# A gated linear attention with an MLP on one core: phase kept as wrapped 16-bit turns, gate preparation in two stages, and a list-scheduled order on all engines but Pool

## Chip, cores and metric

One core of one Trainium2 chip. The metric is the device time of one execution in microseconds (us). The engines are called PE (matrix multiply), DVE (VectorE), ACT (ScalarE), POOL (GpSimd) and SP (the queue that issues most loads). "Busy" and "idle" are read from a hardware profile of one execution.

## The reference, cut to what matters

```
B, H, S, D = 4, 8, 768, 48
mag   = sqrt(a_re^2 + a_im^2);  scale = min(mag, 0.999) / (mag + 1e-6)
a     = (a_re + i a_im) * scale                  # complex gate per position and channel
for t in range(S):
    State = a[t][:, None] * State + outer(k[t], v[t])    # complex 48x48 state per head
    y[t]  = q[t] @ real(State)
x   = y with heads side by side                   # (4, 768, 384)
out = x + relu(layernorm(x) * g_ln @ w_ch1) @ w_ch2      # 384 -> 1536 -> 384
```

The kernels do this in 24 chunks of 128 positions (6 per batch), three chunks to a "group", so eight groups. With the gate in polar form, the product of gates from one position to another is the exponential of a difference of cumulative log magnitudes `l` and a rotation by a difference of cumulative angles `th`. A group's gate preparation makes `e`, `en` (the exponentials of the cumulative logs and of their negatives), `sin` and `cos` of the cumulative angle, and the stacked operands `ks`, `qs` = k or q, times `en` or `e`, times `cos` or `sin`. Attention and the MLP then run on PE.

## The kernel before

The parts that the change touches:

```python
ctx.enter_context(tc.manual_schedule())     # each engine runs in the order of writing

def merge(*lists):                          # one step: attention of chunk n, a third of the
    ...                                     # preparation of the next group, a third of an MLP

# preparation of group g, all of it within the three steps before the group is used
L  = [le1, le2, le3]                        # ACT: w=ln(are), rinv=exp(-w); DVE: r=aim*rinv, r2=r*r
                                            # ACT: u=ln(1+r2); DVE: l=min(0.5u+w, cap)+eps
L += [lambda c=c: le4(c) for c in range(GC)]   # PE: lps=u_f^T l; ACT: e=exp(lps), en=exp(-lps)
L += [decay, tr1]                           # chunk totals; ACT: other table set, th=arctan(r)
L += [lambda c=c: tr2(c) for c in range(GC)]
L += [qk, tr3]                              # POOL: ke=k*en, qe=q*e; ACT: sin, cos
L += [lambda c=c: stack(c) for c in range(GC)]

def tr2(c):                                 # phase in turns, wrapped to [-0.5, 0.5]
    nc.tensor.matmul(ps, lhsT=u_th, rhs=th, start=True, stop=(car is None))
    if car is not None:
        nc.tensor.matmul(ps, lhsT=one_th, rhs=car, start=False, stop=True)
    nc.vector.tensor_scalar(out=n, in0=ps, scalar1=MAGIC, scalar2=MAGIC,
                            op0=ALU.add, op1=ALU.subtract)         # round to whole turns
    nc.vector.tensor_tensor(out=st["f"][:, c], in0=ps, in1=n, op=ALU.subtract)
    ... nc.gpsimd.tensor_tensor(out=nxt, in0=car, in1=th, op=ALU.add)   # running sum of angles
# tr3: af = f & 0x7FFF (DVE); sin = Sin(2 pi f), cos = Sin(pi/2 - 2 pi af) (ACT)

def transp(which):                          # "ks" and "qs"
    ... nc.vector.tensor_copy(out=t, in_=ps)
def mm1(jp):                                # first MLP layer, one double-bank PSUM tile
    ps = ph.tile([C, 2, 512], FP32, tag="h", name="hps")            # ph has one buffer
    ... six matmuls, then nc.scalar.activation(out=st["h"][:, ts(jp, 2)], in_=..., func=AF.Relu)
```

## Time and profile before

| before | |
|---|---|
| median of 4 runs | 347.40 us (345.75 to 348.66) |
| busy, of a span of 345.4 us | PE 215.6, DVE 206.4, ACT 167.9, POOL 93.6 us |
| first transposes of ks on PE | 30.4 us |
| time between the groups' sin activations, from 131 us on | 34 to 39 us |

The page of the kernel before: its span, the busy time of each engine, the busy tenths of PE, DVE and of PE's granted clock in 40 slices of the span, and the chain that ended last by engine.

```profile
span 345.4 us, 4940 instructions
PE 215.6 (62%) x1917; PEld 141.9 (41%) x1917; DVE 206.4 (60%) x424; ACT 167.9 (49%) x254; POOL 93.6 (27%) x115
PE   0041027644635754689568596789467949979884
DVE  1438066997896458837983568456955875743021
PEclk9999998855956788689868967688969989999999
PE 40%; DVE 29%; ACT 14%; SPq 6%; DMA 4%; POOL 3%; issue 2%; DVEq 0%
```

No engine is above two thirds. PE is hardly busy for the first six slices (52 us). Its granted clock is full there (9 in every slice) and at the end, and reduced in most slices between (down to 5). The chain that ended last goes from engine to engine; nothing is a bottleneck by its work. The list of waits says what the engines stood behind (engine and line, what it waited for: us in total, times, longest):

```profile
POOL v L104 <- PE tps L251: 49.6, 2, 26.4
PE lps L213 <- DVE l L206: 56.5, 8, 18.4
PE tp L315 <- DVE ks L291: 19.5, 8, 6.0
DVE w1b L153 <- DMA w1b<-in_moe_w_ch_dram: 8.5, 1, 8.5
```

PE waits for the beginning of the preparation (l) and again for its end (ks), once in each of the eight groups. DVE stood 8.5 us at the start behind a weight that no work of that moment needed. The costs of lines that the change touches, from the groups of instructions (busy us, mean ns of one | idle before, releaser):

```profile
L257 DVE TENSOR_TENSOR f<-tps,n 128x384 f16<-128x384 f32 x24 | 13.4, 558 | 0.8
L317 DVE COPY qsT<-tp 96x1024 bf16<-96x1024 bf16 x24 | 16.4, 684 | 15.0 <-PE tp L315 15.0
L204 DVE SCALAR_TENSOR_TENSOR l<-u,w 128x1152 f16<-128x1152 f16 x8 | 10.8, 1352 | 3.0 <-ACT u L201 2.7
L206 DVE TENSOR_SCALAR l<-l 128x1152 f16<-128x1152 f16 x8 | 3.7, 460 | 0.3
```

The sin activation, once per group, gives the groups' period. From the instructions of ACT in order of time (start us, length us):

```profile
165.01 1.16 ACT L275 ACTIVATE sin<-f 128x1152 bf16<-128x1152 f16 x1 [1.05 <-DVE f L257]
204.15 1.16 ACT L275 ACTIVATE sin<-f 128x1152 bf16<-128x1152 f16 x1
240.65 1.16 ACT L275 ACTIVATE sin<-f 128x1152 bf16<-128x1152 f16 x1 [1.05 <-DVE f L257]
```

### The profile page before, as it was taken

How to read it: one execution, taken by the hardware profiler on the slowest of the kernel's cores; microseconds unless marked ns; L12 is line 12 of the kernel's file. 1: busy time of each engine (PE TensorE's matmuls, PEld its weight loads, DVE VectorE, ACT ScalarE, POOL GpSimd, SP SyncE). 2: the span in 40 equal slices, each digit the busy share in tenths (PEclk: the TensorE clock that was granted, in tenths of full speed). 3: DMA queues.
4: the chain of work that ended last, by engine and by line, in shares of the span. 5: the costliest groups of instructions: out<-in, count | busy, mean ns of one | idle time of the engine just before them, and what ended most of it. 6: DMA issues, size and time to landing. Idle time of an engine off the chain costs nothing.

```text
span 345.4 us, 4940 instructions
## 1 busy us (share of the span) xinstructions
PE 215.6 (62%) x1917; PEld 141.9 (41%) x1917; DVE 206.4 (60%) x424; ACT 167.9 (49%) x254; POOL 93.6 (27%) x115
## 2 busy tenths in 40 slices
PE   0041027644635754689568596789467949979884
PEld 0011014343623543356335363556235727756442
DVE  1438066997896458837983568456955875743021
ACT  5167025255483719365836328373837426363620
POOL 5039203800650076006400391017300820000000
PEclk9999998855956788689868967688969989999999
DMA  9999999997086099000096095910000000001111
GB/s 136 156 189 179 194 172 138 179 189 109 3 149 127 0 54 153 0 25 23 18 195 108 25 68 107 188 30 23 25 0 23 25 23 25 26 25 46 46 47 68
DMA packets 130311, 28.63 MB, mean 83 GB/s; under 512 B 125296, under 2 KB 129904, under 8 KB 130288
## 3 DMA queue, kind: packets, MB, share of 16 engines
q1 hardware_dynamic: 103696, 23.60, 39.2%
q0 software_dynamic: 26592, 4.72, 16.8%
q8 instruction: 15, 0.25, 0.3%
q14 instruction: 8, 0.07, 0.1%
HBM read 28.31 MB, written 4.72 MB: 96 GB/s over the span
## 4 chain that ended last, share of the span: by engine, by line
PE 40%; DVE 29%; ACT 14%; SPq 6%; DMA 4%; POOL 3%; issue 2%; DVEq 0%
PE hps L418 14%; PE o L427 13%; PE tp L315 4%; SPq L97 3%; DMA w1b<-in_moe_w_ch_dram 3%; SPq L89 3%; DVE ks L291 3%; DVE l L204 3%; ACT cos L276 3%; ACT L236 2%; DVE atm L329 2%; DVE qsT L317 2%; DVE qs L292 2%; ACT th L239 2%; PE lps L213 2%
## 5 line engine op out<-in xcount | busy, mean ns | idle before, releaser
L418 PE MATMUL hps<-xT,w1c 128*128 128x384 bf16 x288 | 67.1, 378 | 21.2 <-DVE xT L381 18.5
L421 ACT ACTIVATE h<-hps 128x768 bf16<-128x768 f32 x48 | 38.8, 808 | 71.0 <-PE hps L418 70.5
L427 PE MATMUL o<-w2b,h 128*128 128x384 bf16 x288 | 62.5, 361 | 2.2 <-DVE ot L432 2.2
L418 PEld LDWEIGHTS <-w1c 128*128 128x128 bf16 x288 | 29.9, 110 | 44.8 <-DVE xT L381 17.1
L213 PE MATMUL lps<-l,u_f 128*128 128x384 f16 x24 | 10.3, 448 | 56.5 <-DVE l L206 56.5
L427 PEld LDWEIGHTS <-h 128*128 128x128 bf16 x288 | 31.2, 108 | 27.7 <-issue 13.1
L432 DVE SCALAR_TENSOR_TENSOR ot<-o,rstd,x 128x384 f32<-128x384 f32 x24 | 14.7, 614 | 43.8 <-PE o L427 43.8
L329 DVE TENSOR_TENSOR atm<-at,mask 128x512 bf16<-128x512 f32 x48 | 32.6, 678 | 1.9 <-PE at L327 1.8
L315 PE MATMUL tp<-ident,ks 128*96 128x128 bf16 x192 | 18.7, 254 | 19.5 <-DVE ks L291 19.5
L213 PEld LDWEIGHTS <-u_f 128*128 128x128 f16 x24 | 2.7, 114 | 57.6 <-DVE l L206 41.0
L263 POOL TENSOR_TENSOR car<-th 128x384 f16<-128x384 f16 x4 | 3.6, 909 | 82.9 <-ACT th L239 82.9
L317 DVE COPY qsT<-tp 96x1024 bf16<-96x1024 bf16 x24 | 16.4, 684 | 15.0 <-PE tp L315 15.0
L315 PEld LDWEIGHTS <-ks 128*96 128x96 bf16 x192 | 16.0, 150 | 21.8 <-DVE ks L291 21.4
L293 POOL TENSOR_TENSOR qs<-qe,sin 128x384 bf16<-128x384 bf16 x24 | 22.9, 979 | 7.2 <-issue 5.3
L215 ACT ACTIVATE e<-lps 128x384 bf16<-128x384 f32 x24 | 12.0, 499 | 24.3 <-PE lps L213 24.3
L104 POOL DMA_DIRECT2D v<-in_v_dram x4 | 9.2, 2290 | 50.5 <-PE tps L251 49.6
L263 POOL TENSOR_TENSOR car<-car,th 128x384 f16<-128x384 f16 x12 | 10.9, 909 | 44.0 <-ACT th L239 43.3
L283 POOL TENSOR_TENSOR qe<-q,e 128x384 bf16<-128x384 f32 x24 | 22.1, 946 | 0.0
L283 POOL TENSOR_TENSOR ke<-k,en 128x384 bf16<-128x384 f32 x24 | 21.2, 908 | 0.0
L327 PE MATMUL at<-qsT,ksT 96*128 96x128 bf16 x192 | 20.7, 235 | 0.0
L369 DVE BATCH_NORM_STATS2 stats<-x 128x6 f32<-128x384 bf16 x24 | 13.3, 554 | 12.1 <-ACT x L367 12.1
L194 DVE TENSOR_TENSOR r<-aim,rinv 128x384 f16<-128x384 f32 x24 | 13.2, 550 | 10.4 <-DMA aim<-in_a_im_dram 10.4
(90 smaller groups left out, 447.1 us busy)
## 6 DMA issues: line engine op xcount, KB each, us to landing
are<-in_a_re_dram SPq DMA_DIRECT2D x24, 192.0 KB, 4.2
aim<-in_a_im_dram SPq DMA_DIRECT2D x24, 192.0 KB, 4.6
k<-in_k_dram SPq DMA_DIRECT2D x24, 192.0 KB, 4.5
q<-in_q_dram SPq DMA_DIRECT2D x24, 192.0 KB, 4.6
out_dram<-ot SPq DMA_DIRECT2D x24, 192.0 KB, 1.9
v<-in_v_dram POOLq DMA_DIRECT2D x4, 576.0 KB, 11.9
w1b<-in_moe_w_ch_dram POOLq DMA_DIRECT2D x1, 1152.0 KB, 10.4
w2b<-in_moe_w_ch_dram POOLq DMA_DIRECT2D x1, 1152.0 KB, 17.7
```

The lines of the kernel that those rows point to most:

```text
L213: nc.tensor.matmul(ps, lhsT=u_f, rhs=st["l"][:, c].rearrange("p h d -> p (h d)"), start=True, stop=True)
L263: nc.gpsimd.tensor_tensor(out=nxt, in0=car, in1=th, op=ALU.add)
L283: nc.gpsimd.tensor_tensor(out=t[:, c], in0=st[nm][:, c].rearrange("p h d -> p (h d)"), in1=st[e][:, c], op=ALU.mult)
L293: nc.gpsimd.tensor_tensor(out=st["qs"][:, c, :, 1], in0=qq, in1=st["sin"][:, c], op=ALU.mult)
L315: nc.tensor.transpose(ps[:, h], st[which][:, c, h].rearrange("p a d -> p (a d)"), ident)
L317: nc.vector.tensor_copy(out=t, in_=ps)
L327: nc.tensor.matmul(ps[:, i], lhsT=x["ks"][:, h], rhs=x["qs"][:, h], start=True, stop=True)
L329: nc.vector.tensor_tensor(out=x["atm"][:, ds(half * (H // 2), H // 2)], in0=ps, in1=mask.unsqueeze(1).to_broadcast([C, H // 2, C]), op=ALU ...
L418: nc.tensor.matmul(ps[:, ji, 0:GC * C], lhsT=W["w1c"][:, dc, ts(j, C)], rhs=st["xT"][:, dc].rearrange("p c t -> p (c t)"), start=(dc == 0) ...
L421: nc.scalar.activation(out=st["h"][:, ts(jp, 2)], in_=ps[:, :, 0:GC * C], func=AF.Relu)
L427: nc.tensor.matmul(st["o"], lhsT=st["h"][:, j, ts(c, C)], rhs=W["w2b"][:, j], start=(j == 0), stop=(j == NJ - 1))
L432: nc.vector.scalar_tensor_tensor(out=ot, in0=st["o"], scalar=st["rstd"][:, ds(c, 1)], in1=x["x"], op0=ALU.mult, op1=ALU.add)
```

## The change

Intent, in five parts.

1. Phase. The cumulative turns get 192 added on the way out of PSUM, the memory that PE writes to. A float near 192 has a fixed exponent, so its low 16 bits are the fraction of a turn, as a signed integer. ACT reads those 16 bits directly; rounding, subtracting and masking go. The carry to the next chunk is the last row's fraction (on POOL, 32 partitions), no more a sum of all angles. The cosine becomes 1 - 2 sin^2 of the half angle (two DVE instructions).
2. Two stages. Logs, ratio, `l` and arctan of a group are written one period before the rest of its preparation.
3. Order. Only POOL's order is fixed. The other engines' orders come from a list scheduler, which sets them when the kernel is built, with a written plan as priorities; the activations that need a table set keep their written order by edges.
4. Placement and size. The qsT copies go from DVE to ACT; r, r2 and the stack products are done on 1152 columns at once instead of 384; v gets a third buffer.
5. Start. Group 0 is prepared chunk by chunk; a, k and q of the first groups load before v and the weights.

The diff, cut to its core:

```diff
-    ctx.enter_context(tc.manual_schedule())
+    ctx.enter_context(tc.manual_schedule(engines={mybir.EngineType.Pool}))
...
-        def tr2(c):  ... round, subtract ...   # and tr3: mask, sin, cos
+    def turns(t):
+        return t.bitcast(I16).rearrange("p (x two) -> p x two", two=2)[:, :, 0]
+    def s_phase(g, c, eng=nc.gpsimd):
+        nc.tensor.matmul(ps, lhsT=u_th, rhs=row(G[g]["th"], c), start=True, stop=first)
+        if not first:
+            nc.tensor.matmul(ps, lhsT=last[96:C, :], rhs=X[n - 1]["car"][96:C, :],
+                             start=False, stop=True)
+        nc.vector.tensor_scalar(out=row(ph, c), in0=ps, scalar1=WINDOW, scalar2=None,
+                                op0=ALU.add)                       # WINDOW = 192.0
+            eng.tensor_scalar(out=X[n]["car"][96:C, :], in0=turns(row(ph, c)[96:C]),
+                              scalar1=1.0 / TURN, scalar2=None, op0=ALU.mult)   # 65536
+    def s_sin(g, cs):      # sin and hs = Sin at half the scale, both from the 16 bits
+    def s_cos(g, cs):      # hq = hs*hs;  cos = -2*hq + 1
...
-            nc.vector.tensor_copy(out=t, in_=ps)
+            (nc.scalar.copy if which == "qs" else nc.vector.tensor_copy)(out=t, in_=ps)
...
+    for g in range(2, NG):                     # stage one, a period ahead
+        t = GC * (g - 2)
+        add(t + 0.05, lambda g=g: g_log(g, ALL))
+        add(t + 0.30, lambda g=g: g_ratio(g, ALL))
+        add(t + 1.30, lambda g=g: g_log1p(g, ALL))
+        add(t + 1.40, lambda g=g: g_decay(g, ALL))
+        add(t + 1.55, lambda g=g: g_angle(g, ALL))
+    for g in range(1, NG):                     # stage two
+        t = GC * (g - 1)
+        for c in range(GC):
+            add(t + 0.10 + 0.2 * c, lambda g=g, c=c: s_phase(g, c))
+            add(t + 0.20 + 0.3 * c, lambda g=g, c=c: s_decay(g, c))
+            add(t + 0.50 + 0.3 * c, lambda g=g, c=c: s_scale(g, "k", c))   # POOL
+            add(t + 1.40 + 0.3 * c, lambda g=g, c=c: s_scale(g, "q", c))   # POOL
+        add(t + 1.60, lambda g=g: s_sin(g, ALL))
+        ... s_cos, s_stack (q by sin on POOL, the rest on DVE)
+    for g in range(NG):                        # MLP of group g: steps 3g+5 to 3g+8
+        plan.spread(GC * g + 5, GC * g + 6.5, L1)
+        plan.spread(GC * g + 6.5, GC * g + 8, L2)
```

## The prediction

> **What bounds it now.** No engine: the page's busy shares are PE 215.6 us (62%), DVE 206.4, ACT 167.9, POOL 93.6 of 345.4. The chain of waits is mixed (PE 40%, DVE 29%, ACT 14%), so the cost is fixed program order, where each engine stands behind one late item.
> - Start: the instructions in order of time show the first ks transposes at 30.4 us, then DVE idle from 34.9 to 43.5 us behind the w1b load (8.5 us in the list of waits); PE is nearly idle until 50 us.
> - Middle: the cos activation recurs at 132, 166, 207, 242 and 276 us, about 35 us per group of three chunks. The busy table for 153 to 187 us: PE 25.0, DVE 23.9, ACT 19.9, POOL 9.8 of 34. A group's gate preparation is one serial chain inside its own period (logs, l, cumulative matmul, exps, table switch, arctan, phase, sin, cos, stacking); lps waited 56.5 us for l in all, transposes 19.5 us for ks.
> - End: after 297 us, 48 us, mostly the MLP of more than two groups alone on PE (84 first-layer and 120 second-layer matmuls).
>
> **What changes, in work.**
> - DVE: the subtraction f (13.4 us) and af (4.5) go; the 24 qsT copies (16.4) move to ACT; ks and qs products are fused from 384 to 1152 columns, as are r and r2 (estimate -15 us together). Added: hq (est. 0.7 us x8) and cos as tensor_scalar (0.46 like l's x8). The Trainium skill ("VectorE: DVE Perf Modes", side-by-side table) gives 16-bit tensor_scalar the 4x rate; l's 0.46 us for 1152 agrees. DVE estimate: 206 to about 163 us.
> - ACT: +24 qsT evictions of 1024 columns, about 1.05 us each (interpolated from 0.50 for 384 and 0.81 for 768): +25; one row exp fewer per group (-3.4); fused logs (-4). Estimate 168 to 186.
> - POOL: about 88.
> - PE: about the same matmuls. But in "TensorE: Matmul & The Clock Gate" (Part 1) idleness re-throttles the clock; here the granted clock was 0.68 at 140-150 us and 1.00 at 290-300 us where PE never idled. A denser PE should gain: 215 to about 195 us.
>
> **What changes, in waiting.** This is the main gain. Stage one (logs, l, arctan) runs a period ahead, breaking the serial chain; list scheduling takes away most standing behind late items; the MLP lag is about 29 steps instead of 33; v has a third buffer, so POOL's v issue (49.6 us waiting for tps) no longer holds POOL. At start v and the weights load after a, k and q, and group 0 goes chunk by chunk.
>
> **Sum.** First transposes at about 26 us with no long stall after; eight groups at about 29 us (PE or ACT at 23-25 busy, times 1.2); about 20 us for the last chunk and last MLP: 26 + 232 + 20 = 278, plus a little for early DMA shortage (130-190 GB/s until 90 us).
>
> **Predicted: 282 us, 80% range 260 to 306.** Faster by over 2%: 0.95; within 2%: 0.03; slower: 0.02.
>
> **What would show it.** DVE near 163, ACT near 186; period of the sin activation 27-31 us; PE clock above 0.9; chain with over 50% PE; tail after the last stacking about 25 us; w1b wait gone.
>
> **What would make it wrong.** A scheduler whose assumed durations are off gives static orders with new standing still, above all at weights arriving later than it assumed; the five PSUM buffers limiting run-ahead; single-buffered gate tiles tying stage two to the previous group; POOL's fixed order; early DMA limiting the first three groups.

## The result, and the profile after

The changed kernel takes 280.84 us (median of 4 runs, 278.57 to 281.85) against 347.40 us. The ratio is 0.8077, with a 95% interval of 0.8018 to 0.8137. Ratios here are the mean time of one kernel's runs over that of the other's in the same rounds, so they are not quite the ratio of the medians quoted. Executions over 1.5% slower than the fastest of the same kernel are left out of the means.

The same lines of the page of the changed kernel:

```profile
span 279.1 us, 4840 instructions
PE 207.4 (74%) x1915; PEld 136.4 (49%) x1917; DVE 197.2 (71%) x328; ACT 175.4 (63%) x247; POOL 99.3 (36%) x107
PE   0321542747849996989799969988998999998673
DVE  0679906999699669986997699689848946633001
PEclk9999999999786998999799979997999999999999
PE 33%; DVE 32%; ACT 12%; issue 11%; POOL 8%; DMA 2%; POOLq 0%; DVEq 0%; ACTq 0%
```

Every engine's busy time is within 10 us of before, in a span that is 66 us shorter. The gain is not work but standing. PE is dense from the thirteenth slice on (84 us), and its mean granted clock rose from 0.865 to 0.957. What the clock adds to the gain is not shown: two of the four runs of the changed kernel had 0.906 and 0.908 and were no slower. The waits for l and ks that came back eight times have shrunk to single events, and the wait for w1b does not appear:

```profile
PE lps L246 <- DVE l L232: 10.6, 1, 10.6
PE tp L320 <- DVE ks L307: 1.7, 1, 1.7
```

The period of the sin activation is now 27.0 to 27.2 us in the middle (26.5 us on average over all six):

```profile
133.97 1.17 ACT L196 ACTIVATE sin<-ph 128x1152 bf16<-128x1152 int16 x1
161.14 1.17 ACT L196 ACTIVATE sin<-ph 128x1152 bf16<-128x1152 int16 x1
188.11 1.17 ACT L196 ACTIVATE sin<-ph 128x1152 bf16<-128x1152 int16 x1
```

Something unexpected stands in the groups of instructions. The two instructions that make l, untouched in the text, cost DVE 43.0 us instead of 14.5 ("+1 forms" mixes in the three chunk-wise ones of group 0). The carry costs POOL 1.3 us each, the qsT copies ACT 1.0 us each:

```profile
L230 DVE SCALAR_TENSOR_TENSOR l<-u,w 128x1152 f16<-128x1152 f16 (+1 forms) x10 | 28.8, 2886 | 3.0 <-ACT u L196 3.0
L232 DVE TENSOR_SCALAR l<-l 128x1152 f16<-128x1152 f16 (+1 forms) x10 | 14.2, 1431 | 0.1
L281 POOL TENSOR_SCALAR car<-ph 32x384 f16<-32x384 int16 x17 | 22.1, 1300 | 79.6 <-DVE ph L277 78.5
L322 ACT COPY qsT<-tp 96x1024 bf16<-96x1024 bf16 x24 | 24.1, 1004 | 7.8 <-PE tp L320 7.8
```

Side by side in order of time, DVE's l and what POOL does meanwhile (one group of the middle; start us, length us):

```profile
103.37 4.09 DVE L230 SCALAR_TENSOR_TENSOR l<-u,w 128x1152 f16<-128x1152 f16 x1 [0.39 <-ACT u L196]
109.17 1.80 DVE L232 TENSOR_SCALAR l<-l 128x1152 f16<-128x1152 f16 x1
```
```profile
103.59 2.65 POOL L301 TENSOR_TENSOR qe<-q,e 128x384 bf16<-128x384 f32 x3
108.29 2.36 POOL L307 TENSOR_TENSOR qs<-qe,sin 128x1152 bf16<-128x1152 bf16 x1 [2.05 <-ACT sin L196]
```

The first l took 1.35 us in the kernel before. Here it starts while POOL ends a product of k, then stands through POOL's three back-to-back products of q, and ends 1.2 us after the last. The second, 0.46 us before, ends 0.3 us after POOL's next product. That is the theory of experiment 6. The one l of 1152 columns in this kernel that met no product on POOL took its old time:

```profile
78.19 1.33 DVE L230 SCALAR_TENSOR_TENSOR l<-u,w 128x1152 f16<-128x1152 f16 x1
```

The kernel before already had the same effect, on smaller instructions. Eleven of its 72 products of 128x384 on DVE took 1.06 instead of 0.35 us, all of them while POOL multiplied. One of them, and what POOL did meanwhile:

```profile
30.31 1.06 DVE L292 TENSOR_TENSOR qs<-qe,cos 128x384 bf16<-128x384 bf16 x1
```
```profile
30.13 2.99 POOL L293 TENSOR_TENSOR qs<-qe,sin 128x384 bf16<-128x384 bf16 x3
```

The end is the other unexpected thing. The last ks and qs products are done at 222 us, and 57 us follow. From 239 to 268 us the chain that ended last is PE and ACT taking turns on the one PSUM tile of the first MLP layer:

```profile
240.35 0.82 ACT h L410
...
241.21 1.14 PE hps L407 x6
...
243.30 1.09 PE hps L407 x6
244.42 0.82 ACT h L410
```

### The profile page after: what moved, and what is told of

The parts are those of the page before. It is cut to its first block, busy times and chain, and to the rows that moved or that the text cites. A ratio compares the mean times of both kernels' runs of the same rounds, so it can differ in the third digit from the quotient of the medians.

```text
span 279.1 us, 4840 instructions
## 1 busy us (share of the span) xinstructions
PE 207.4 (74%) x1915; PEld 136.4 (49%) x1917; DVE 197.2 (71%) x328; ACT 175.4 (63%) x247; POOL 99.3 (36%) x107
## 4 chain that ended last, share of the span: by engine, by line
PE 33%; DVE 32%; ACT 12%; issue 11%; POOL 8%; DMA 2%; POOLq 0%; DVEq 0%; ACTq 0%
PE o L416 14%; PE hps L407 10%; DVE l L230 7%; POOL car L281 6%; ACT h L410 4%; DVE atm L334 3%; DVE ot L421 3%; DVE ks L307 2%; DVE l L232 2%; DVE stats L371 2%; DVE qs L307 2%; ACT u L196 2%; DVE ph L277 2%; DVE hq L295 1%; PE tot L254 1%
## 5 line engine op out<-in xcount | busy, mean ns | idle before, releaser
L410 ACT ACTIVATE h<-hps 128x768 bf16<-128x768 f32 x48 | 38.8, 809 | 49.4 <-PE hps L407 49.1
L407 PE MATMUL hps<-xT,w1c 128*128 128x384 bf16 x288 | 55.9, 330 | 4.7 <-ACT h L410 3.8
L281 POOL TENSOR_SCALAR car<-ph 32x384 f16<-32x384 int16 x17 | 22.1, 1300 | 79.6 <-DVE ph L277 78.5
L230 DVE SCALAR_TENSOR_TENSOR l<-u,w 128x1152 f16<-128x1152 f16 (+1 forms) x10 | 28.8, 2886 | 3.0 <-ACT u L196 3.0
L322 ACT COPY qsT<-tp 96x1024 bf16<-96x1024 bf16 x24 | 24.1, 1004 | 7.8 <-PE tp L320 7.8
L220 DVE TENSOR_TENSOR r<-aim,rinv 128x1152 f16<-128x1152 f32 (+1 forms) x10 | 11.1, 1111 | 16.9 <-DMA aim<-in_a_im_dram 10.1
L307 POOL TENSOR_TENSOR qs<-qe,sin 128x1152 bf16<-128x1152 bf16 x7 | 16.9, 2418 | 11.9 <-ACT sin L196 11.9
L332 PEld LDWEIGHTS <-ksT 96*128 96x128 bf16 x192 | 15.2, 104 | 10.4 <-issue 7.9
L322 DVE COPY ksT<-tp 96x1024 bf16<-96x1024 bf16 x24 | 16.3, 681 | 4.4 <-PE tp L320 4.3
L320 PE MATMUL tp<-ident,qs 128*96 128x128 bf16 x192 | 18.7, 238 | 0.2 <-ACT x L369 0.2
L320 PEld LDWEIGHTS <-qs 128*96 128x96 bf16 x192 | 16.1, 137 | 5.6 <-issue 3.5
```

Source lines behind the costliest of these rows:

```text
L230: nc.vector.scalar_tensor_tensor(out=cut(l, cs), in0=cut(G[g]["u"], cs), scalar=0.5, in1=cut(G[g]["w"], cs), op0=ALU.mult, op1=ALU.add)
L281: eng.tensor_scalar(out=X[n]["car"][96:C, :], in0=turns(row(ph, c)[96:C]), scalar1=1.0 / TURN, scalar2=None, op0=ALU.mult)
L307: eng.tensor_tensor(out=t[:, cs, :, a].rearrange("p c h d -> p (c h) d"), in0=heads(G[g][which + "e"]), in1=heads(G[g]["sin" if a else "co ...
L320: nc.tensor.transpose(ps[:, h], st[which][:, c, h].rearrange("p a d -> p (a d)"), ident)
L322: (nc.scalar.copy if which == "qs" else nc.vector.tensor_copy)(out=t, in_=ps)
L332: nc.tensor.matmul(ps[:, i], lhsT=x["ks"][:, h], rhs=x["qs"][:, h], start=True, stop=True)
```

## The experiments

Twelve kernels ran, each timed in three rounds beside the kernel before, which gave 347 us each time. The chips differ between sets of runs, so kernels of different sets are best compared by their ratios to before. All but one (e11) gave correct results. The first four take the change apart.

### 1. The kernel before, list-scheduled

```diff
-    ctx.enter_context(tc.manual_schedule())
+    ctx.enter_context(tc.manual_schedule(engines={mybir.EngineType.Pool}))
+    # table loads and Ln/Exp/Arctan/Sin activations chained by no-sync edges
```

> The kernel before, with one thing of the change: only the Pool order is fixed, the rest is list-scheduled (the logarithm, exponential and trigonometric activations keep their written order by no-sync edges, as in the changed kernel). Theory A, that standing behind late items in a fixed order was the main cost: 305 to 325 us, at least a third of the 66 us gain. Rival B, that the gain comes from the two-stage preparation and its new plan, and list scheduling without slack in the dependences finds nothing to reorder: within 2% of before, 340 to 352 us.

Measured: 307.17 us, ratio 0.889 (0.8841 to 0.894). Theory A holds: letting go of the fixed order, with the arithmetic and the plan of before, takes off 40 us by itself.

### 2. The changed kernel, with every order fixed

```diff
-    ctx.enter_context(tc.manual_schedule(engines={mybir.EngineType.Pool}))
+    ctx.enter_context(tc.manual_schedule())
-        if chained: tc.add_manual_dep(...)      # not needed, and not allowed, there
```

> The changed kernel with every engine's order fixed to the order in which the plan writes it (the edges between activations become needless and go). Theory A: 300 to 325 us, since the plan's positions are rough and every engine again stands behind late items. Rival B (the plan and the two stages make the gain, the scheduler only polishes): 282 to 295 us.

Measured: 294.45 us, ratio 0.8496 (0.8456 to 0.8537). One of the four runs was slow (298.75 us); the median of the other three is 293.82 us, and the ratio leaves it out. Here the rival's range was hit. So each theory is right in its own kernel: with the old plan the scheduler is worth 40 us, with all else changed 14. The separate gains (40 us for the scheduler, 52 for all the rest) add up to more than 66, so in part they remove the same time.

### 3. The changed kernel with the old phase

```diff
-        tensor_scalar(ph = ps + 192); car from the 16 bits; sin, hs; hq, cos on DVE
+        n = round(ps); f = ps - n; af = f & 0x7FFF        # DVE
+        car = car + th on POOL; matmul(one_th, car); sin, cos on ACT
```

> The changed kernel with the old phase arithmetic: round-and-subtract, and-mask, cosine as an activation with a bias, carry as a running sum of angles on Pool with a full matmul. Adds about 13.4 us (f) and 4 us (af) to DVE and takes off hq 6.3 and cos 3.9; Pool carry 14 instead of 22 us, and the carry no longer hangs from the phase of the chunk before. If DVE is what binds the middle: 285 to 292 us. If the chain through the carry costs more than DVE's work: 276 to 281 us.

Measured: 279.79 us, ratio 0.8078 (0.8038 to 0.8119), against 0.8077 for the changed kernel. The part that names the change gives nothing by itself in this kernel. DVE was busy 202.0 us instead of 197.2, so it did have more to do, and the time did not move. The second expectation is the one that was met; what the carry costs is the subject of experiment 12.

### 4. The changed kernel with one stage

```diff
-        t = GC * (g - 2)
+        t = GC * (g - 1)          # logs .. l just before stage two, arctan and phases
+                                  # behind the switch to the trigonometric tables
```

> The changed kernel with stage one of a group's gate preparation (logs, ratio, decay, arctan) moved from the period before into the same period as stage two, loads of a moved with it. If the two stages are what made the middle dense: period of the sin activation 32 us or more, 305 to 325 us. If list scheduling alone does it: within 2%, 277 to 286 us.

Measured: 307.59 us, ratio 0.8895 (0.8847 to 0.8944). The sin activations are 30.2 to 34.0 us apart from 115 us on (31.7 on average, just under the 32 expected), and the expected time is met. Together with experiment 1 this gives one split. From before (347) to list-scheduled (307) to everything else but the two stages (308) to the two stages (281): 40, 0 and 27 us. The new phase, the moved copies, the wider products and the new start are all in the step that is worth nothing in sum; single gains and losses in it can cancel (experiment 12 finds one such pair). In another order of adding the shares differ, as experiment 2 shows.

The list of waits of this kernel shows what came back. ACT stands for the phase inside the period, and PE stands once more for the stacked ks, seven times (eight before):

```profile
ACT sin L196 <- DVE ph L277: 33.5, 8, 8.8
PE tp L320 <- DVE ks L307: 15.8, 7, 3.5
```

### 5. qsT back on DVE

```diff
-            (nc.scalar.copy if which == "qs" else nc.vector.tensor_copy)(out=t, in_=ps)
+            nc.vector.tensor_copy(out=t, in_=ps)
```

> The changed kernel with the 24 qsT copies back on VectorE (0.68 us each there, 1.00 on ScalarE): DVE +16 us, ACT -24 us. If VectorE is near its limit in the middle (about 9 of 10 busy in half of the 10 us windows): 286 to 296 us. If PE alone binds: 278 to 283 us.

Measured: 282.27 us, ratio 0.8134 (0.8093 to 0.8175), which overlaps the changed kernel's interval. DVE was busy 206.8 us, ACT 154.9. Ten more us of busy DVE, with twenty less of ACT, cost nothing that can be told from zero, so DVE's total alone is not what binds. "PE alone binds" does not follow: the next experiment shortens the time with PE's work unchanged.

### 6. q's scaling off POOL

```diff
-        nc.gpsimd.tensor_tensor(out=row(t, c), ...)
+        eng = nc.vector if which == "q" and g else nc.gpsimd
+        eng.tensor_tensor(out=row(t, c), ...)
```

> The changed kernel with the scaling of q by its decay on VectorE instead of Pool for groups 1 to 7 (21 products of 128x384). Theory: l's two VectorE instructions take 4.1 and 1.8 us instead of 1.35 and 0.46 because each lasts until Pool's back-to-back instruction run ends. With the q products off Pool the first of them should fall to 1.35 to 1.6 us (its mean from 2.9 to below 1.9 over all forms), DVE total within 6 us of before the edit although it has 12 us of work more. Rival (l is slow for another reason, such as the types or the ScalarE neighbour): l stays at 4.1 and DVE grows by 12 us. Time: 274 to 283 us by the theory, above 284 by the rival.

Measured: 270.61 us, ratio 0.7779 (0.7733 to 0.7826), better than the range expected. The groups of instructions of this kernel:

```profile
L230 DVE SCALAR_TENSOR_TENSOR l<-u,w 128x1152 f16<-128x1152 f16 (+1 forms) x10 | 15.8, 1588 | 2.5 <-ACT u L196 2.5
L232 DVE TENSOR_SCALAR l<-l 128x1152 f16<-128x1152 f16 (+1 forms) x10 | 4.8, 485 | 0.1
L308 DVE TENSOR_TENSOR ks<-ke,sin 128x1152 bf16<-128x1152 bf16 (+1 forms) x10 | 16.8, 1684 | 0.3 <-ACT sin L196 0.2
```

l is back at 1.33 to 1.47 us and 0.45 us from the second l of 1152 columns on, and DVE's total is the same 197.2 us with the q products' 12.7 us more on it. The rival is out. The same standing moved to another instruction: ks by sin, which now meets POOL's sine product of q, went from 0.76 to 1.68 us on average. In order of time, DVE's ks by sin and POOL's qs by sin of one group:

```profile
105.60 2.49 DVE L308 TENSOR_TENSOR ks<-ke,sin 128x1152 bf16<-128x1152 bf16 x1
```
```profile
105.11 2.36 POOL L308 TENSOR_TENSOR qs<-qe,sin 128x1152 bf16<-128x1152 bf16 x1 [4.60 <-ACT sin L196]
```

The Trainium skill ("GPSIMD Engine Reference", Key points) says that GpSimd "shares its SBUF interfaces with VectorE — contention with DVE instructions in a 2-port perf mode or with two SBUF inputs". This trace agrees. The first l and ks by sin read two SBUF tensors. The second l has one input and takes 0.46 us undisturbed for 1152 columns; at the 0.96 GHz of the skill's page "VectorE: DVE Perf Modes" (Specifications) that is an estimated 2.6 columns per cycle, more than any mode gives there that does not use both ports (side-by-side table). The DVE instructions that read PSUM and one SBUF tensor kept their length: in the changed kernel, atm took its usual 0.68 us at 76.9 us, under POOL's products of q.

### 7. The first MLP layer of the last group in single banks

```diff
+            if g == NG - 1:
+                for j in (jp * 2, jp * 2 + 1):
+                    ps = pa.tile([C, 512], FP32, tag="a", name="hp1")    # one of five buffers
+                    ... three matmuls; Relu on DVE for odd j, on ACT for even j
+                return
```

> The changed kernel, with the first MLP layer of the last group alone written in single-bank tiles from the pool of five, evicted in turns by ScalarE and VectorE, instead of through the one double-bank tile. In the tail of the changed kernel six matmuls (1.15 us) and one eviction (0.82 us) take turns from 239 to 268 us. Theory: this turn-taking is what makes the tail long, and 7 to 12 us go: 269 to 274 us. Rival: the tail is PE's work: within 1%.

Measured: 275.20 us, ratio 0.7913 (0.7858 to 0.7969). 5.6 us go by the medians, so the turn-taking was part of the long end (the edit also gives half of the Relus to DVE, which is not separated). That is less than the 7 to 12 us expected, and the rest of the end remains.

### 8. Experiments 6 and 7 together

> The two edits that helped, together: q scaled on VectorE for groups 1 to 7, and the last group's first MLP layer in single-bank tiles. They touch different stretches (10.2 us and 5.6 us by the medians of the single runs), so they should add: 263 to 268 us. If the earlier finish of the middle only moves work into the same tail: 268 to 271 us.

The edit is the sum of the two shown. Measured: 264.58 us, ratio 0.7608 (0.7559 to 0.7656). They add.

### 9. As 8, with l of group 1 behind group 0's phase

```diff
+        if g == 1:      # l after the third phase instruction of group 0, on DVE
+            tc.add_manual_dep(ins.ins, X[GC - 1]["ph_ins"].ins.name, ...NoSync...)
```

> As e8_qscale_tail, with group 1's decay l put behind the three phase instructions of group 0 on VectorE by an edge. In the changed kernel this l stood ahead of them and took 5.8 us under Pool's products, from 17.4 to 23.2 us, while group 0's phase was due at about 19.6 us. Theory (VectorE's order binds the start): first transposes at 27 instead of 32.6 us and 3 to 5 us less than e8. Rival (loads bind the first 90 us): the first transposes come earlier, the second group does not, and the time stays within 1% of e8.

Measured: 267.40 us, ratio 0.7704 (0.7664 to 0.7745), 1.1% worse than 8 on the same chip. Neither range was met: the theory's gain did not come, and the rival's 1% was just missed. The first transposes came at 28.7 instead of 32.3 us, near the 27 hoped for, and the second group's sin came later, at 56.3 instead of 52.3 us. Why is seen on DVE in order of time:

```profile
46.22 1.36 DVE L220 TENSOR_TENSOR r<-aim,rinv 128x1152 f16<-128x1152 f32 x1 [6.03 <-DMA aim<-in_a_im_dram]
47.49 0.55 DVE L280 TENSOR_SCALAR ph<-tps 128x384 f32<-128x384 f32 x1
```

The scheduler had put r of group 2, whose input was still loading, in front of group 1's second phase. On the chip that order stood 6 us behind the load, and the carry and all that hangs from it stood with it. The changed kernel has the same order there, with r at 42.35 us after 7.8 us of waiting; in this run the load landed 4 us later still, which was not looked into. A list-scheduled order is as fixed as a written one once it is built.

### 10. As 9, with the carry and q's sine product off POOL

```diff
-    def s_phase(g, c, eng=nc.gpsimd):
+    def s_phase(g, c, eng=nc.vector):
-        s_stack(g, "q", 1, ALL, nc.gpsimd)
+        s_stack(g, "q", 1, ALL, nc.vector)
```

> As e9_start_l, with the carry and the sine product of q on VectorE too, so that Pool keeps the k products and small copies alone. VectorE has about 12 us of work more (20 x 0.36 and 7 x 0.74) and should lose about 10 us of standing (ks by sin at 1.7 us mean should fall to 0.65, hq and cos to 0.6 and 0.39). Theory that standing and work cancel: within 1.5% of e9. If the carry's hop over Pool (1.17 us, 8 us of PE waits) is what holds the middle: 4 us or more below e9.

Measured: 254.94 us, ratio 0.7335 (0.7298 to 0.7373), 12.5 us below 9. The first expectation failed, and the size of the second was exceeded; that the carry's hop is the cause does not follow, since the edit moves two things. DVE's work and standing did cancel, 197.9 us busy against 196.4, but the time did not stay. The two profiled executions are 15.3 us apart. Of these, 6.9 us are won at the start: group 1's sin comes at 49.4 instead of 56.3 us. Without the hop over POOL the scheduler put all phases of group 1 before the late r. On DVE in order of time:

```profile
33.63 0.56 DVE L280 TENSOR_SCALAR ph<-tps 128x384 f32<-128x384 f32 x1 [0.24 <-PE tps L278]
35.98 0.56 DVE L280 TENSOR_SCALAR ph<-tps 128x384 f32<-128x384 f32 x1 [1.40 <-PE tps L278]
43.16 1.34 DVE L220 TENSOR_TENSOR r<-aim,rinv 128x1152 f16<-128x1152 f32 x1
```

Another 6.3 us come in the middle, where the period of the sin activation fell from 25.0 to 23.4 us. This is the best kernel. Its page:

```profile
span 251.7 us, 4820 instructions
PE 198.9 (79%) x1917; PEld 132.5 (53%) x1917; DVE 197.9 (79%) x379; ACT 173.3 (69%) x247; POOL 45.3 (18%) x62
PE   0304385638585999989999999999999999997983
```

PE is at nine tenths in almost every slice of the middle, so little standing of PE is left to remove there. The start, to slice 13 (82 us), is what remains.

### 11. The changed kernel without the loads of q

```diff
-        for name, ap in (("k", k), ("q", q)):
+        for name, ap in (("k", k),):
+        st["q"] = st["k"]                       # wrong result on purpose
```

> Gives a wrong result on purpose: the changed kernel with k's tile read in place of q, so 4.7 of 28.3 MB read are not loaded; no other instruction changes. If loads bind the first 90 us (130 to 220 GB/s there): groups 1 to 3 come earlier and 4 to 8 us go, 273 to 277 us. If not: 279 to 282 us.

Measured: 280.44 us, ratio 0.8086, so no change. The first large sins came at 51.8, 77.6 and 106.2 us (52.4, 78.4 and 107.0 with q), so a sixth less to load did not bring the groups forward by 1 us. That the amount of loads binds is not supported, but the run does not settle it. The scheduler built another order, in which another late item takes the place: DVE stood 8.3 us behind w1b, where the changed kernel stood 7.8 us behind the input of r. In the list of waits of this kernel:

```profile
DVE w1b L160 <- DMA w1b<-in_moe_w_ch_dram: 8.3, 1, 8.3
```

### 12. The changed kernel with the carry on DVE

```diff
-    def s_phase(g, c, eng=nc.gpsimd):
+    def s_phase(g, c, eng=nc.vector):
```

> The changed kernel with one edit: the carry from chunk to chunk on VectorE (0.36 us each undisturbed) instead of Pool (1.17 us or more each), for all groups. Theory that the carry's hop over Pool, in Pool's fixed order and with the next chunk's phase hanging from it, costs the new phase its gain: 270 to 277 us, and most of what e10_pool_empty won over e9_start_l is the carry. Rival: the win of e10 came from taking the sine product of q off Pool as well, and here the l instructions still stand 4 us behind Pool's q products: 279 to 284 us.

Measured: 274.85 us, ratio 0.7904 (0.7875 to 0.7934), inside the first range, 6 us below the changed kernel and, by the ratios, as much below the old phase of experiment 3. So with its carry on DVE the new phase beats the old one as it was, and with the carry on POOL it did not. Experiment 3 had its running sum on POOL too; the old phase with that sum on DVE was not run, so a gain of the new arithmetic itself is not shown. DVE was busy 207.2 us, ten more, and l still stood behind POOL (2.6 us mean). Here too the scheduler put group 1's phases (the last at 37.0 instead of 46.4 us) before the late r. Group 2's sin then came 2.6 us earlier, and the rest of the gain built up over the later groups. Whether that rest comes from the shorter hop in the chain of carries or from meeting POOL less is not separated. The first part of the expectation is met; that most of the 12.5 us of experiment 10 is the carry is not shown, since this run had another base.

## Why the prediction was right

The time (282 against 280.84 us) and the main reason were right. That the number is so close is luck: its terms missed in both directions. The start to the first transposes was 6.6 us longer than in the sum, the stretch from there to the last stack products 13 us shorter, and the end 8 us longer.

- "The cost is fixed program order", and waiting is "the main gain": right. Experiments 1 and 4 give 40 us for the scheduler and then 27 us for the two stages, and nothing for all the rest in sum.
- Period "about 29 us" (27 to 31): it is 27.0 us, at the lower edge. From the first transposes (32.6 us) to the last stack products (222.2 us) it took 189.6 us, where seven periods of the sum are 203.
- "First transposes at about 26 us": 32.6 us. DVE's l of group 1 stood in front for 5.8 us. And PE was not dense until 84 us: "no long stall after" was wrong. Experiments 9 and 11 show orders standing behind loads there.
- "About 20 us for the last chunk and last MLP", after eight periods: from the last stack products on the sum had 29 + 20 = 49 us, and it took 57. The text's other figure, "tail after the last stacking about 25 us", does not agree with its own sum and was wrong. Turn-taking on one PSUM tile is 5.6 us of it (experiment 7).
- DVE "206 to about 163 us": wrong by 34 us. The single terms that were named came out near their size. f, af and qsT went (-34.3), the wider products gave -16.7 against -15 estimated, hq and cos cost +10.2, the carry of group 0 +2.1; that makes 168. What was missing is +28.5 us of l standing behind POOL. No line of l in the profile before has this cost, since POOL was idle whenever l ran, but the stack products at 1.06 us had it. Those eleven cost about 8 us more than undisturbed ones (11 times 0.71), so nearly half of the -16.7 is less standing and not width, and that term was right partly by luck. Experiment 6 showed the cause.
- ACT "168 to 186": 175.4. The copies cost 24.1 us as estimated (25). Fewer table loads (19 instead of 22, at 1.283 us each) and lower logs made up for part.
- POOL "about 88": 99.3. The carries alone cost 22.1 us on POOL, where the running sums of before had cost 14.5.
- PE's clock "above 0.9": 0.957. The skill ("TensorE: Matmul & The Clock Gate", Part 1) says that idleness throttles the clock. The profiled runs fit in the mean, with PE denser and the clock up from 0.865, but not slice by slice: in the kernel before the clock was full in the first 52 us, with PE nearly idle. "215 to about 195 us" busy was too much, 207.4.
- "Chain with over 50% PE": 33%. The chain still changed from engine to engine, and experiments 6, 10 and 12 show what stood in it: DVE held up by POOL, and the carry.
- Of the listed dangers, "new standing still" at late loads did happen (experiments 9 and 11), and "POOL's fixed order" or at least its work was the largest cost left (6, 10, 12). "Early DMA" by amount was not one (11).

What stays open: how much of what experiment 10 won in the middle is the hop of the carry and how much the interference with POOL; whether its edge from experiment 9 helps or harms it; whether the old phase would gain as much with its running sum on DVE; and why ten more us of DVE work cost nothing in experiment 5.

## What to carry to other kernels

When no engine is above two thirds busy and the chain hops between engines, order and slack are worth more than arithmetic: here 40 and then 27 us came from these two, and nothing measurable from the arithmetic saved, with the carry where the change put it. Before moving two-input products to an idle POOL, look at what DVE runs at that moment; what matters is not POOL's busy share but which DVE instruction has to stand behind it. A scheduler's order is fixed once built, so keep instructions that need a late load away from the front of a chain.

## What the Trainium skill lacked or had wrong

- No page, "GPSIMD Engine Reference" (Key points) and "SBUF — State Buffer" (Who interferes with whom) included, says how long a DVE instruction waits when POOL's instructions follow back to back. Here l stood through three in a row (1.35 became 4.09 us, with 2.65 us of POOL) and at the start through what was left of six (5.81 us), and got in between none of them. In the kernel before, products of 384 columns did get in between (0.35 became 1.06 us, about one to each POOL product). What decides between the two is not shown.
- "GPSIMD Engine Reference" (Engine selection) has one-input elementwise work on GpSimd roughly at line rate. POOL's carry, one input, 32x384 from 16-bit integers at every second place, took 1.167 us at the least, more than a two-input product of 128x384 there (0.90 us); DVE did the same carry in 0.356 us. Whether the stride, the type or the 32 partitions makes it slow was not separated.
- No page has a time for ScalarE reading 16-bit integers at a stride of two ("SBUF — State Buffer" has a general note on strides, with its cachelines, and no figure for this engine). It cost nothing that can be seen: 1.16 us for 1152 columns, as for dense 16-bit floats before (1.16 us).
